# Windowed attention re-ordered into steps of two blocks, ahead of a mixture-of-experts layer, on one Trainium2 core

## The chip, the core and the metric

The kernel runs on one core of one Trainium2 chip. The core has five engines that run on their own and meet at semaphores: PE (TensorE, matmuls and transposes), ACT (ScalarE), DVE (VectorE), POOL (GpSimd) and SP (SyncE, which here only issues transfers). Matmul results land in PSUM, which has eight banks of 512 fp32 columns; operands come from SBUF. The metric is the device time of one execution in microseconds (us).

## What is computed

Four sequences of 768 tokens, eight heads of 64. Each query sees the keys of its last `n_local` = 96 positions and the first `n_global` = 8, with a bias that falls with distance; softmax, then the weighted sum of the values. The 3072 rows of 512 that result go through a cosine router that picks one of eight experts for each row, and the expert's two matmuls.

```python
scores = scale * q @ k.T + bias; a = exp(scores - max); a /= sum(a) + 1e-9
x = (a @ v) as rows of 512                       # 3072 x 512
logits = (x / |x|) @ (emb / |emb|).T / tau       # 8 experts
e = argmax(logits); gate = softmax(logits)[e]
out[row] = gate * (relu(x[row] @ w1[e]) @ w2[e]) # 512 -> 1024 -> 512, fp32
```

## The kernel before, in words

**Attention.** A group is one sequence and four heads (two pairs of heads); there are eight groups, two to a sequence. A unit is one block of 96 keys plus up to 30 global keys (126 rows) against 192 queries; a group has eight units, and there are 64. For each group, `turn` transposes k and q (three transposes into a PSUM bank, one copy by ACT; eight turns for a group). For each unit, `score` issues four matmuls into one tile of two PSUM banks, `sp`, of which there is one; ACT takes the exponential of both banks in one operation (L344); DVE multiplies by a table of biases in two operations (L350). `attend` then adds the values' product into banks `od` (L370) and the sums of the weights into a third (L376, a matmul with ones). After four blocks ACT and DVE copy the three banks out to `xd`.

**Router.** For each of the six row tiles of a sequence (a chunk), `sums` multiplies `xd` with the experts' embedding (L408), transposes the weight sums (L411) and the previous chunk's products (L413), and DVE makes reciprocals and logits of them; `rows` transposes x (L433), DVE scales it, SP stores it to DRAM, ACT squares and sums it. When a sequence is done (the last one in two halves), `choose` finds the expert, the slot of each row, and scatters row numbers and gates to DRAM with six transfers issued by POOL (L202).

**Experts.** For each expert the rows are gathered by number (L643), transposed (L656), multiplied by w1 (L694) and w2 (L666), and scattered to the output (L670).

**What sets the order.** In the attention a scheduler orders the instructions of every engine by priority and readiness, from a program that issues for unit i its scores, one turn of the next group, one router task and the attend of unit i-1. PSUM is divided as two banks for `sp`, four for `od`, two for all else. POOL copies the global rows of v to all eight blocks (L314). All loads go through SP's queue, the first q through ACT's. The program of the experts is issued in the order in which it is written. In the trace each fp32 matmul shows as two rows, so a unit's four score matmuls are eight rows; a transpose is one row.

Of the kernel before, what the change touches and what calls it, by code (L numbers as in the profile page):

```python
# [16 lines left out]
ARMS = (PE, mybir.EngineType.Activation, mybir.EngineType.DVE, mybir.EngineType.Pool)  # L17

# [59 lines left out]
def load_numbers(k, n_global, n_local):  # L78
# [3 lines left out]
    for i, ap in enumerate((n_global, n_local)):  # L82
        nc.scalar.dma_start(raw[:, i, :], ap.bitcast(I32).partition_broadcast(P))
    words = pool.tile([P, 2, 2], F32, name="words")
# [7 lines left out]
    k.ng, k.nl = num[:, 0:1], num[:, 1:2]  # L92

# [12 lines left out]
def prep_expert_emb(k, emb_in, tau, ps):  # L106
# [6 lines left out]
    nc.sync.dma_start(emb[:], emb_in[:, :])  # L113
    sq = pool.tile([E, k.DM], F32, name="emb_sq")
# [4 lines left out]
    nc.gpsimd.tensor_tensor(out=ss[:], in0=ss[:], in1=tau_sb[:], op=ALU.mult)  # L119
    nc.vector.reciprocal(out=ss[:], in_=ss[:])  # L120
    nc.vector.tensor_scalar_mul(emb[:], emb[:], ss[:])
    k.en = pool.tile([P, k.NC, E], F32, name="en")
# [3 lines left out]
    k.enb = pool.tile([P, k.NC, 32], F32, name="enb")  # L126
    nc.gpsimd.memset(k.enb[:], 0.0)
# [5 lines left out]
def load_weights(k, e, w):  # L133
    nc = k.nc
    nc.sync.dma_start(w[0][:], k.w1[e].rearrange("(c p) f -> p c f", p=P))
    nc.sync.dma_start(w[1][:], k.w2[e].rearrange("(f p) m -> p f m", p=P))

# [10 lines left out]
def choose(k, b, i0, n, lg, ss, pool, cp):  # L148
# [21 lines left out]


# [10 lines left out]

    both = new([2, n, E], "both")
# [17 lines left out]
    for t in range(n):  # L201
# [5 lines left out]
        if k.scatters is not None:  # L207
# [3 lines left out]
            k.scatters.append(i.ins)  # L211


def route(k, b, xb, pool):
# [18 lines left out]
    choose(k, b, 0, NT, lg, ss, pool, k.work.tile([P, 512], F32, name="work", tag="work"))  # L233
# [5 lines left out]
def window_table(k, tmp):  # L239
# [9 lines left out]
    rel, far, loc, t = new("rel"), new("far"), new("loc"), new("t")  # L249
# [9 lines left out]
    nc.vector.tensor_scalar(out=t[:], in0=rel[:], scalar1=0.0, scalar2=None, op0=ALU.is_ge)  # L259
    nc.vector.scalar_tensor_tensor(out=loc[:], in0=rel[:], scalar=k.nl, in1=t[:],  # L260
# [13 lines left out]
    for m in range(2):  # L274
        for e in range(2):
            for a in range(2):
                nc.scalar.activation(k.table[:, m, e, a], rel[:], AF.Exp, scale=-k.slopes[4 * m + 2 * a + e])


def window_attention(k, ctx):  # L280
# [71 lines left out]
    def attend(u):  # L352
# [34 lines left out]
        if jj == QB - 1 and n > BLK:  # L387
            g.od = g.od2
# [495 lines left out]
```

## Time and profile before

| | us |
|---|---|
| runs: median of 3 (lowest to highest) | 688.64 (681.72 to 688.98) |
| the profiled execution, its time | 687.63 |
| its span, first to last instruction | 685.8 |
| PE busy in the span | 605.1 (88%) |
| DVE, ACT, POOL busy | 178.6, 141.9, 110.6 |

Times in the profile count from the first instruction. The span has a start (0 to 19.57), the attention proper (to 256.42, the last matmul with the ones), a tail in which the last rows are routed and the first expert's rows gathered (to 297.61), and the experts (to 670.32, the last matmul). A busy PE is not PE at its peak: matmuls are pipelined, and the clock that the chip grants to PE (PEclk) is 1.00 at 2.4 GHz and 0.50 at 1.2 GHz.

### The profile page before, as it was taken

Reading aid. Unit: us, or ns where it says so; the run is one execution under the profiler, and the core shown is the slowest. Engines: PE = TensorE matmul, PEld = TensorE weight load, DVE = VectorE, ACT = ScalarE, POOL = GpSimd, SP = SyncE. Lnnn points to the kernel's source line nnn. Section 1 sums busy time; section 2 is a strip of 40 time slices with the busy share of each in tenths; the row PEclk is TensorE's granted clock in tenths of the full one; section 3 lists DMA queues with packets and bytes.
Section 4 is the critical chain, followed back from the end, with each engine's and each line's share of the span. In section 5 each row is a group of like instructions: output and inputs, shape, how many; then the busy total and the mean of one; then the engine's idle time right before and its main releaser. Section 6 shows DMA issues by size and latency. Waiting matters only on the chain.

```text
span 685.8 us, 8692 instructions
## 1 busy us (share of the span) xinstructions
PE 605.1 (88%) x3314; PEld 338.0 (49%) x3314; DVE 178.6 (26%) x509; ACT 141.9 (21%) x280; POOL 110.6 (16%) x146
## 2 busy tenths in 40 slices
PE   4889998599879984089999999999999999999990
PEld 3556664356546652055456444465564554444540
DVE  3434555255635656011001101001011010020000
ACT  3544552245235431001001011010010100100100
POOL 3110103100310032330130120130301203011010
PEclk9999998979899996579999999999999999999996
DMA  9936783854101028130444150453432535101000
GB/s 228 227 83 153 227 232 90 53 134 106 37 16 47 33 45 293 26 104 1 140 162 169 62 183 1 172 203 141 153 133 80 200 140 174 44 19 48 0 31 22
DMA packets 102685, 75.69 MB, mean 110 GB/s; under 512 B 83441, under 2 KB 83569, under 8 KB 102523
## 3 DMA queue, kind: packets, MB, share of 16 engines
q1 hardware_dynamic: 93610, 58.44, 31.0%
q0 software_dynamic: 5488, 14.71, 5.9%
q8 instruction: 52, 0.85, 0.6%
q10 hardware_dynamic: 3424, 0.79, 0.5%
q14 instruction: 111, 0.90, 0.5%
HBM read 61.11 MB, written 13.59 MB: 109 GB/s over the span
## 4 chain that ended last, share of the span: by engine, by line
PE 56%; DMA 3%; DVE 1%; POOL 1%; issue 0%; ACT 0%; POOLq 0%; SPq 0%; ACTq 0%
PE work L666 27%; PE big L694 25%; PE work L656 2%; DMA x_dram<-xs 1%; DMA meta<-mt,slot 1%; DMA xg<-x_dram,ids 1%; DMA emt<-meta 0%; POOL xg L643 0%; PE tp L433 0%; PE tp L408 0%; PE tp L411 0%; PE od L370 0%; POOL out_dram L670 0%; PE od L376 0%; DVE y L669 0%
## 5 line engine op out<-in xcount | busy, mean ns | idle before, releaser
L666 PE MATMUL work<-w2t,hT 128*128 128x512 f32 x432 | 187.4, 594 | 0.0
L694 PE MATMUL big<-xT,w1t 128*128 128x320 f32 (+5 forms) x512 | 173.6, 500 | 0.8 <-DVE xT L657 0.8
L694 PEld LDWEIGHTS big<-xT,w1t 128*128 128x128 f32 x512 | 98.1, 192 | 76.2 <-issue 42.2
L666 PEld LDWEIGHTS work<-w2t,hT 128*128 128x128 f32 x432 | 81.5, 190 | 101.0 <-issue 99.5
L696 ACT ACTIVATE hT<-big 128x640 f32<-128x640 f32 (+5 forms) x32 | 26.6, 830 | 353.0 <-PE big L694 353.0
L350 DVE TENSOR_TENSOR ex<-ex,table 126x384 f32<-126x384 f32 (+1 forms) x128 | 68.8, 575 | 91.9 <-ACT ex L344 83.8
L670 POOL DMA_INDIRECT out_dram<-y,ids x27 | 26.8, 993 | 301.4 <-DVE y L669 228.7
L340 PE MATMUL sp<-qT,kT 64*126 64x192 f32 (+1 forms) x512 | 67.0, 364 | 7.2 <-ACT qT L328 4.9
L370 PE MATMUL od<-ex,v 126*64 126x192 f32 (+1 forms) x576 | 63.6, 325 | 7.6 <-POOL mt L200 3.8
L669 DVE TENSOR_SCALAR y<-work,emt 128x512 f32<-128x512 f32 x27 | 20.3, 751 | 185.2 <-PE work L666 185.2
L344 ACT ACTIVATE ex<-sp 126x768 f32<-126x768 f32 x64 | 49.2, 768 | 83.9 <-PE sp L340 63.9
L657 DVE COPY xT<-work 128x512 f32<-128x512 f32 x32 | 20.2, 684 | 157.9 <-PE work L656 157.9
L340 PEld LDWEIGHTS sp<-qT,kT 64*126 64x126 f32 x512 | 43.8, 196 | 27.7 <-issue 14.4
L370 PEld LDWEIGHTS od<-ex,v 126*64 126x64 f32 x576 | 35.1, 141 | 27.8 <-issue 16.9
L376 PE MATMUL od<-ex,ones 126*32 126x192 f32 (+1 forms) x576 | 36.7, 318 | 0.7 <-issue 0.7
L656 PE MATMUL work<-ident,xg 128*128 128x128 f32 x128 | 19.0, 295 | 20.7 <-DMA xg<-x_dram,ids 20.7
L643 POOL DMA_INDIRECT xg<-x_dram,ids x32 | 30.9, 966 | 24.0 <-DVE ids L639 14.9
L202 POOL DMA_INDIRECT meta<-mt,slot x24 | 23.9, 996 | 43.9 <-DVE slot L193 19.1
L656 PEld LDWEIGHTS work<-ident,xg 128*128 128x128 f32 x128 | 15.4, 151 | 25.6 <-DMA xg<-x_dram,ids 21.1
L314 POOL COPY v<-v 30x1792 f32<-30x1792 f32 x8 | 13.6, 1706 | 70.5 <-DMA v<-in_v_dram 70.3
L323 PE MATMUL tp<-ident,k 128*128 128x128 f32 x96 | 20.1, 334 | 5.5 <-DMA k<-in_k_dram 5.5
L433 PE MATMUL tp<-ident,xd 128*128 128x128 f32 x96 | 16.4, 299 | 8.8 <-DVE lh L423 8.3
(117 smaller groups left out, 300.3 us busy)
## 6 DMA issues: line engine op xcount, KB each, us to landing
w1t<-in_moe_w_dram SPq DMA_DIRECT2D x8, 2048.0 KB, 9.9
w2t<-in_moe_w_dram SPq DMA_DIRECT2D x8, 2048.0 KB, 12.4
k<-in_k_dram SPq DMA_DIRECT2D x32, 192.0 KB, 3.2
v<-in_v_dram SPq DMA_DIRECT2D x32, 192.0 KB, 3.4
x_dram<-xs SPq DMA_DIRECT2D x24, 256.0 KB, 6.1
q<-in_q_dram SPq DMA_DIRECT2D x28, 192.0 KB, 3.4
q<-in_q_dram ACTq DMA_DIRECT2D x4, 192.0 KB, 4.9
xg<-x_dram,ids POOLq DMA_INDIRECT x32
```

The source lines that it names most:

```text
L202: i = nc.gpsimd.indirect_dma_start(out=k.meta[:], out_offset=bass.IndirectOffsetOnAxis(ap=slot[:, t : t + 1], axis=0), in_=mt[:, t, :], in ...
L340: nc.tensor.matmul(sp[0:ROWS, e, a * n : (a + 1) * n], lhsT=t.kT[rows, j, 0:ROWS], rhs=t.qT[rows, j * BLK : j * BLK + n], start=True, stop ...
L344: nc.scalar.activation(ex, sp[0:ROWS, :, 0 : 2 * n], AF.Exp, scale=k.scale)
L350: nc.vector.tensor_tensor(out=exv, in0=exv, in1=tb, op=ALU.mult)
L370: nc.tensor.matmul(od[a][e * D : (e + 1) * D, cols], lhsT=g.v[0:ROWS, 2 * a + e, j, :], rhs=ex[:, e, a * n + c0 : a * n + c1], start=first ...
L376: nc.tensor.matmul(od[2][32 * i : 32 * i + 32, cols], lhsT=k.ones[0:ROWS, 0:32], rhs=ex[:, e, a * n + c0 : a * n + c1], start=first, stop= ...
L643: nc.gpsimd.indirect_dma_start(out=xg[:], out_offset=None, in_=k.x_dram[:], in_offset=bass.IndirectOffsetOnAxis(ap=ids[:, j : j + 1], axis=0),
L656: k.nc.tensor.transpose(ps[:, c, :], xg[:, c * P : (c + 1) * P], k.ident[:])
L666: nc.tensor.matmul(ps[:], lhsT=hT[:, f, j * P : (j + 1) * P], rhs=w2[:, f, :], start=f == 0, stop=f == k.NF - 1)
L670: nc.gpsimd.indirect_dma_start(out=k.out[:, :], out_offset=bass.IndirectOffsetOnAxis(ap=ids[:, j : j + 1], axis=0), in_=y[:], in_offset=No ...
L694: nc.tensor.matmul(ps[:, i, 0:w], lhsT=w1[:, c, f * P : (f + 1) * P], rhs=xT[:, c, 0:w], start=c == 0, stop=c == k.NC - 1)
L696: nc.scalar.activation(hT[:, 2 * f2 : 2 * f2 + 2, 0:w], ps[:, :, 0:w], AF.Relu)
```

## The change

The attention is written out in steps. One step takes two units: the four matmuls of the first unit's scores, the four of the second, then all transposes that are due (turns, x of a chunk, weight sums), then the attend of the previous step's two units with all products with v first and all products with ones after, then the chunk's product with the embedding. There are 32 steps, four to a group, and some more for what is left of the router. The order of PE, ACT, DVE and SP is that of the program (`manual_schedule`); POOL's is still the scheduler's. PSUM is divided anew: five single banks in rotation for scores, turns and chunks, three for `od`. The exponential is now one operation for each bank, the table's multiplication one for each unit. `choose` and the preparation of the embedding are cut into parts that are issued a step apart. The global rows of v come by transfers from DRAM, and POOL's copies are gone. The first group's k and q are loaded in halves ahead of all else, the bias table is made in two halves, the first expert's weights are loaded in eight parts over steps 9 to 23, and the second expert's weights wait for that expert's row gathers.

```diff
-    sp_p, od_p, tp_p = (pool("wa_sp", 1, space=PSUM), pool("wa_od", 4, space=PSUM),
-                        pool("wa_tp", 2, space=PSUM))
+    pa_p, po_p = pool("wa_pa", 5, space=PSUM), pool("wa_po", 1, space=PSUM)
...
-        nc.gpsimd.tensor_copy(out=d[BLK:ROWS, :, 1:NB, :],
-                              in_=d[BLK:ROWS, :, 0:1, :].to_broadcast([GLB, 4, NB - 1, D]))
+    def load_v(g, hs):
+        for h in hs:
+            src = k.v[g.b, 4 * g.m + h]
+            nc.sync.dma_start(g.v[0:BLK, h], src.rearrange("(j r) d -> r j d", r=BLK))
+            nc.sync.dma_start(g.v[BLK:ROWS, h], src[0:GLB].unsqueeze(1).to_broadcast([GLB, NB, D]))
...
-        nc.scalar.activation(ex, sp[0:ROWS, :, 0 : 2 * n], AF.Exp, scale=k.scale)
+    def grow(u, e):
+        nc.scalar.activation(u.ex[:, e], u.sp[e][0:ROWS, 0 : 2 * u.n].rearrange("p (a c) -> p a c", a=2), AF.Exp,
+                             scale=k.scale)
+
+    def weigh(u):
+        kind = min(u.j, 2)
+        tab = k.table[0:ROWS, u.g.m].rearrange("p e a i c -> p (e a) i c")[:, :, kind::(3 - kind), :]
+        exv = u.ex.rearrange("p e a (i c) -> p (e a) i c", c=BLK)
+        nc.vector.tensor_tensor(out=exv, in0=exv, in1=tab[:, :, 0 : u.n // BLK, :], op=ALU.mult)
...
+    numbers = load_numbers(k, k.n_global, k.n_local)
+    for r0, r1 in ((0, 3), (3, 6)):
+        for a in range(2):
+            load_tokens(nc.sync, first.pairs[a].k, k.k, 0, a, r0, r1)
+            load_tokens(nc.scalar, first.pairs[a].q, k.q, 0, a, r0, r1)
+        if r0 == 0:
+            next(numbers)
...
+            us = g.units[2 * p : 2 * p + 2]
+            for u in us:
+                score(u)
+            grow(us[0], 0)
+            grow(us[0], 1)
+            if s == 0:
+                next(table)
+            weigh(us[0])
+            grow(us[1], 0)
+            todo = list(turns[s])
+            if todo:
+                turn(*todo.pop(0))
+            grow(us[1], 1)
+            for x in todo:
+                turn(*x)
...
+        chunk = ready.pop(0) if ready else None
+        if chunk:
+            t, i = chunk
+            xp = turn_x(t, i) if i < NT else None
+            sp = turn_sums(t, i)
+            if xp is not None:
+                store_x(t, i, xp)
+        if routers:
+            try:
+                next(routers[0])
+            except StopIteration:
+                routers.pop(0)
+        if going:
+            weigh(us[1])
+        if 1 <= s <= 4 * len(groups):
+            q = groups[(s - 1) // 4]
+            attend(q, (s - 1) % 4)
...
+        if chunk and i < NT:
+            score_experts(t, i, sp)
...
-        with ExitStack() as inner:
+        with tc.manual_schedule(engines=ORDERED), ExitStack() as inner:
             window_attention(n, inner)
...
-                load_weights(n, e, t.w)
+                load_weights(n, e, t.w, n.gathers if e == 1 else ())
```

On PE, inside the attention, two units before (`sp`: scores, `od`: products with v and with ones, `tp`: transposes and products with the embedding; counts are matmuls):

```order
L408 MATMUL tp<-xd,enb 32x128 x4
L411 MATMUL tp<-ident,xd 128x128 x2
L413 MATMUL tp<-ident,lS 128x128
L370 MATMUL od<-ex,v 64x192 x4
L376 MATMUL od<-ex,ones 32x192 x4
L340 MATMUL sp<-qT,kT 126x192 x4
L323 MATMUL tp<-ident,k 128x128 x3
L433 MATMUL tp<-ident,xd 128x128 x4
L370 MATMUL od<-ex,v 64x96 x4
L376 MATMUL od<-ex,ones 32x96 x4
```

and one step of the change (`pa`: the five single banks; of the four L421 rows of a full step two stand here):

```order
L395 MATMUL pa<-qT,kT 126x192 x8
L376 MATMUL pa<-ident,k 128x128 x3
L376 MATMUL pa<-ident,q 128x128 x3
L477 MATMUL pa<-ident,xd 128x128 x4
L456 MATMUL pa<-ident,xd 128x128 x2
L458 MATMUL pa<-ident,lS 128x128
L421 MATMUL od_912<-ex,v 64x192 x2
L421 MATMUL od_913<-ex,v 64x192 x2
L429 MATMUL od_914<-ex,ones 32x192 x8
L494 MATMUL pa<-xd,enb 32x128 x4
```

The kinds of matmul now stand in five runs for two units where each unit had four to six runs of its own.

On ACT, at the start, before (`raw`: the numbers n_global and n_local, `table`: the bias table; rows of other copies are left out here and below):

```order
L83 DMA raw_63<-in_n_global_dram 128x2
L83 DMA raw_63<-in_n_local_dram 128x2
L303 DMA q_121<-in_q_dram 128x6x64 x2
L303 DMA q_129<-in_q_dram 128x6x64 x2
L325 COPY kT_125<-tp_173 128x4x96
L328 COPY qT_124<-tp_184 128x384
L277 ACTIVATE table_117<-rel_144 128x384 x8
L328 COPY qT_132<-tp_205 128x384
```

and in the change:

```order
L344 DMA q_109<-in_q_dram 128x3x64 x2
L84 DMA raw_128<-in_n_global_dram 128x2
L84 DMA raw_128<-in_n_local_dram 128x2
L344 DMA q_105<-in_q_dram 128x3x64 x2
L381 COPY qT_110<-pa_250 128x384
L399 ACTIVATE ex_273<-pa_271 126x384
L399 ACTIVATE ex_273<-pa_272 126x384
L309 ACTIVATE table_103<-w_rel_183 128x384 x4
L399 ACTIVATE ex_280<-pa_278 126x384
L381 COPY qT_106<-pa_293 128x384
```

The numbers are now requested behind the first four halves of q, and half of the table is made behind the first unit's exponentials and no longer ahead of the last copies of q.

On POOL, around the first `choose`, before:

```order
L314 COPY v_774<-v_774 30x4x448
L158 TENSOR_TENSOR ss_288<-ss_288,half_244 128x6
L314 COPY v_1096<-v_1096 30x4x448
L200 COPY mt_1850<-tokid_251 128x6
L202 DMA meta_61<-mt_1201,slot_1196 24576x2 x6
L314 COPY v_1425<-v_1425 30x4x448
```

and in the change:

```order
L182 TENSOR_TENSOR ss_265<-ss_265,half_181 128x6
L226 COPY mt_2150<-tokid_220 128x6
L228 DMA meta_61<-mt_1490,slot_1485 24576x2 x6
L182 TENSOR_TENSOR ss_778<-ss_778,half_181 128x6
```

No copy of v stands between the router's instructions on POOL any more.

## Rows read from the trace of the kernel before

**Rows 1.** The page: the chain that ended last, by line.

```profile
PE work L666 27%; PE big L694 25%; PE work L656 2%; DMA x_dram<-xs 1%; DMA meta<-mt,slot 1%; DMA xg<-x_dram,ids 1%; DMA emt<-meta 0%; POOL xg L643 0%; PE tp L433 0%; PE tp L408 0%; PE tp L411 0%; PE od L370 0%; POOL out_dram L670 0%; PE od L376 0%; DVE y L669 0%
```

**Rows 2.** Stretches: start:end length, each engine's busy time (instructions), PEclk, DMA share, GB/s.

```profile
19.57:256.42 236.85, 212.06 (x2162) 132.02 (x2162) 119.67 (x340) 103.31 (x219) 35.42 (x37) 0.94 0.45 104
53.00:78.00 25.00, 25.00 (x281) 15.65 (x277) 12.82 (x26) 12.81 (x28) 1.91 (x1) 1.00 0.75 201
145.00:170.00 25.00, 25.00 (x286) 16.02 (x284) 14.28 (x40) 13.10 (x31) 0.00 (x0) 1.00 0.47 122
205.00:245.00 40.00, 39.93 (x445) 25.12 (x444) 25.57 (x85) 19.71 (x42) 3.86 (x5) 0.99 0.09 34
256.42:297.61 41.19, 12.23 (x71) 8.04 (x67) 15.06 (x86) 3.42 (x12) 11.68 (x13) 0.59 0.52 152
297.61:670.32 372.71, 372.71 (x1058) 192.53 (x1058) 37.40 (x62) 26.57 (x32) 55.83 (x74) 0.99 0.31 107
```

**Rows 3.** Waits of PE in the attention: who for whom, us, times, longest.

```profile
PE tp L433 <- DVE lh L423: 8.3, 1, 8.3
PE od L370 <- POOL mt L200: 3.8, 2, 1.9
PE od L370 <- issue: 3.3, 3, 2.2
```

**Rows 4.** Timeline of ACT: start, length, what, idle before it and its releaser.

```profile
138.08 0.27 ACT L416 COPY lS<-tp 128x128 f32<-128x128 f32 x1 [10.32 <-remote]
```

**Rows 5.** Stretches at the lower clock in the attention: the first, and all five.

```profile
45.47:48.88 3.41, 3.41 (x15) 2.31 (x16) 0.00 (x0) 2.54 (x6) 2.00 (x3) 0.50 0.65 147
...
sum 30.71, PE 25.57 PEld 16.68 DVE 13.87 ACT 12.16 POOL 3.18; mean PE 5.12 PEld 3.33 DVE 2.77 ACT 2.43 POOL 0.64
```

**Rows 6.** Timeline of PE in a dense stretch: start, length, line, form, rows.

```profile
151.21 0.87 PE L370 MATMUL od<-ex,v 126*64 126x192 f32 x8
152.01 0.53 PE L376 MATMUL od<-ex,ones 126*32 126x192 f32 x8
152.47 0.92 PE L340 MATMUL sp<-qT,kT 64*126 64x192 f32 x8
153.32 0.55 PE L323 MATMUL tp<-ident,k 128*128 128x128 f32 x3
153.71 0.60 PE L433 MATMUL tp<-ident,xd 128*128 128x128 f32 x4
154.24 0.55 PE L370 MATMUL od<-ex,v 126*64 126x96 f32 x8
154.72 0.37 PE L376 MATMUL od<-ex,ones 126*32 126x96 f32 x8
155.02 0.39 PE L370 MATMUL od<-ex,v 126*64 126x96 f32 x4
155.34 0.59 PE L340 MATMUL sp<-qT,kT 64*126 64x192 f32 x4
155.86 0.39 PE L370 MATMUL od<-ex,v 126*64 126x96 f32 x4
```

**Rows 7.** Groups of ACT from 145 to 170: busy us, mean ns, idle before.

```profile
L344 ACT ACTIVATE ex<-sp 126x768 f32<-126x768 f32 x7 | 5.7, 807 | 7.6 <-PE sp L340 7.5
L344 ACT ACTIVATE ex<-sp 126x384 f32<-126x384 f32 x1 | 0.5, 471 | 0.0
```

**Rows 8.** Timeline of DVE and ACT at the start: the numbers, the table.

```profile
5.06 0.17 DVE L85 CAST words<-raw 128x4 f32<-128x4 int32 x1 [3.97 <-DMA raw<-in_n_local_dram]
11.52 0.36 DVE L259 TENSOR_SCALAR t<-rel 128x384 f32<-128x384 f32 x1 [5.20 <-POOL rel L254]
15.74 3.41 ACT L277 ACTIVATE table<-rel 128x384 f32<-128x384 f32 x8 [2.94 <-DVE rel L273]
```

**Rows 9.** The chain in order of time, in the tail: start, length, what.

```profile
266.77 10.23 DMA x_dram<-xs
...
277.30 6.71 DMA meta<-mt,slot
```

More of the change, by code (lines that the diff above doesn't have):

```diff
@@ L232, in route @@
         nc.vector.tensor_copy(out=lg[:, t, :], in_=lp[:, 0:E])
-    choose(k, b, 0, NT, lg, ss, pool, k.work.tile([P, 512], F32, name="work", tag="work"))
+    steps = choose(k, b, 0, NT, lg, ss, pool)
+    next(steps)
+    steps.send(k.work.tile([P, 512], F32, name="work", tag="work"))
+    next(steps)
 def window_table(k, tmp):
@@ L334, in score @@
         j, n = u.j, u.n
[L335 removed]
+        u.sp = [bank() for _ in range(2)]
+        u.ex = ex_p.tile([P, 2, 2, 2 * BLK], F32, name="ex", tag="ex")
+        u.ex = u.ex[0:ROWS, :, :, 0:n]
         for a in range(2):
@@ L372, in attend @@
                                      skip_group_check=True)
+        for u, at, c0, c1, first in parts:
             for a in range(2):
@@ L441, in rows, with score_experts @@
         nc.scalar.activation(sq[:], flat, AF.Square, accum_out=t.ss[:, i : i + 1])
-    def finish(t, i0, n):
-        if i0 + n == NT:
-            sums(t, NT)
-        choose(k, t.b, i0, n, t.lg, t.ss, rt_p, bank())
+    def score_experts(t, i, ps):
+        c = slice((i % 3) * P, (i % 3 + 1) * P)
+        for a in range(4):
+            nc.tensor.matmul(ps[32 * a : 32 * a + 32, 3 * P : 4 * P], lhsT=k.enb[:, a, :],
+                             rhs=t.groups[a // 2].xd[i // 3][:, a % 2, c], start=True, stop=True)
+        t.lS[i] = xs_p.tile([P, P], F32, name="lS", tag="lS")
+        nc.scalar.copy(out=t.lS[i][:], in_=ps[:, 3 * P : 4 * P])
+    def finish(t, i0, n):
+        steps = choose(k, t.b, i0, n, t.lg, t.ss, rt_p)
+        next(steps)
+        yield
+        steps.send(bank())
+        yield
+        next(steps)
         if i0 + n == NT:
@@ new lines, in window_attention @@
+    first = groups[0]
+    open_group(first)
+    numbers = load_numbers(k, k.n_global, k.n_local)
+    build_consts(k)
+    for r0, r1 in ((0, 3), (3, 6)):
[4 more added lines that the diff above has]
+            next(numbers)
+    warm = const.tile([P, 1], F32, name="warm")
+    nc.scalar.activation(warm[:], k.ones[:, 0:1], AF.Exp)
+    load_v(first, range(4))
@@ L521, in window_attention, with turns_of @@
-    while tasks:
-        tasks.pop(0)()
+    table = window_table(k, tmp)
+    next(table)
+    next(numbers)
+    next(table)
+    check_numbers(k)
+    build_route_consts(k)
+    for i in (0, 2):
+        for a in range(2):
+            turn(first.pairs[a], i)
+    def turns_of(g, order):
+        return [(g.pairs[a], i) for a in range(2) for i in order]
+    turns = [[] for _ in range(4 * len(groups))]
+    turns[0] = [(first.pairs[a], 3) for a in range(2)]
+    turns[1] = [(first.pairs[a], 1) for a in range(2)]
```

268 lines of the change are left out of this document (136 added, 132 removed).

## The prediction, made before the changed kernel was run

> **What bounds the kernel now.** I read the chain that ended last first. It is PE's work in the experts, L666 and L694, and almost nothing of the attention [rows 1]: the chain is followed back only to where transfers of the tail carry it. So I cut the span into stretches. In the last of them, the experts, PE is busy for all of 372.71 us [rows 2]; nothing there is changed, so these 372.7 us and the 15.5 us behind them stay. The attention takes 236.85 us and the tail 41.19 [rows 2]. What the change can give is in the first 256.42 us.
>
> Is PE the bound there? In three stretches without a wait PE issues 281, 286 and 445 rows in 25, 25 and 40 us [rows 2]: 1012 rows in 90 us, 11.24 a microsecond, at PEclk 1.00 or 0.99. All 2162 rows of the attention at that rate would take 192.3 us. DVE is busy for 0.57 and ACT for 0.52 of the second stretch, so PE is the bound where nothing waits. The other 44.5 us are waits and a slow clock. PE idles 8.3 us for one DVE operation, 3.8 us for `mt` on POOL, 3.3 us for nothing that the profile shows [rows 3]. In 30.71 us PEclk is 0.50, and PE is busy for 25.57 of them [rows 5], which costs half, 12.8 us. These are 28.2 us; about 16 us are many smaller waits.
>
> **The merged runs.** PE's timeline shows that changing from one kind of matmul to another costs time [rows 6]. Eight score rows take 153.32 - 152.47 = 0.85 us, four take 155.86 - 155.34 = 0.52; the second four cost 0.33 and the first four 0.52, so a run costs 0.19 beside its stream. For the products with v, eight rows of 96 columns take 154.72 - 154.24 = 0.48 and four take 155.34 - 155.02 = 0.32: 0.16 a run. For the products with ones, eight rows of 192 take 152.47 - 152.01 = 0.46, of 96 155.02 - 154.72 = 0.30; half of the columns is 0.16, all are 0.32, and 0.14 is left for the run. Three and four transposes in a row take 0.39 and 0.53, 0.92 for seven; the extra one of the second costs 0.14 at most, 0.11 if the run costs 0.15, which I take.
>
> Counts come from the code and from the order that the scheduler made. Scores: 64 runs before, and 8 of them cut in two by an `od` run, so 72; now 32; 40 x 0.19 = 7.6 us. Products with v: ten runs a group, 80, now 32; 48 x 0.16 = 7.7. With ones: nine a group, 72, now 32; 40 x 0.14 = 5.6. Transposes: 64 turns and 24 runs of weight sums behind a product with the embedding, 88, now one a step, 32; 56 x 0.15 = 8.4. The products with the embedding stay 24 runs. Sum 29.3 us, and the dense attention is 192.3 - 29.3 = 163.0. Ends: nothing, if a run of sixteen rows pays at its middle what it paid at its start, and 35 us, if the smaller waits between runs of the old order go too. I take 29.
>
> **What must keep up.** DVE and ACT do the same work in less time: 0.57 x 192.3/163 = 0.67 and 0.52 x 192.3/163 = 0.61. The exponential in two halves costs 2 x 0.471 - 0.807 = 0.135 us more a unit [rows 7], 8.6 us over 64, another 0.05 of ACT. Neither is full, and the products run a step behind their scores, so an exponential has a whole step of about 5 us. I cost the single banks, the split exponential and the five-bank rotation at nothing; PE's own runs hide them. If they were bare, each step would show the ACT time between a score and the reuse of its bank, some 1 us, or 32 us. The parts of `choose` stand on DVE ahead of the second unit's table. One whole `choose` lies in the third stretch, and DVE is at 0.64 there [rows 2], 0.75 after the merge. I take 1 us for each of the four sequences, 4 us; ends 0 and 12.
>
> **The waits.** The 3.8 us for `mt` go: `mt` stands behind the copies of v on POOL, and PE's products with v wait for those copies. Those rows come by 32 more transfers on SP; each also stands ahead of later loads, and DMA is busy for 0.45 of the attention, 107 us [rows 2]. The pieces of 30 x 8 rows are 60 KB each, 1.9 MB in all; at the second row's 201 GB/s for a share of 0.75, 268 GB/s when full, they add 7 us, and 114 us in 163 is 0.70. They are hidden unless loads run late. The waits of PE for `choose` go, because its matmuls are issued a step after their input. With the waits go most of the slow stretches behind them. What I can't explain may come again: the 8.3 us, in which ACT waited 10.32 us for a semaphore that no instruction of the trace set [rows 4], and the 3.3 us. I take half, 6 us, and 3 for the clock behind them; ends 0 and 18. With 4 for `choose` and 2 for loads of the second group that PE may meet in its order, 15 us.
>
> **The start.** Before, the numbers arrived at 5.06, the table's chain ran on DVE from 11.52 (it waited for POOL, which sat behind a copy of v), and ACT made the table from 15.74 to 19.15 [rows 8]; the dense part began at 19.57. Now the numbers are requested behind the first halves of q, and their transfer shares semaphores with those, so I put them 3.5 us later, at 8.5; the DVE chain of 15.74 - 11.52 = 4.2 us then ends near 13.5 with its first operations, half of the table takes 1.7, and the exponentials and q copies behind it 1.8: the second step starts at 17.0 (ends 14 and 20). The first step's 2.3 us of scores and turns are done by then. PE has been mostly idle, so the first microseconds run at the lower clock: 3 us more.
>
> **The tail.** The chain there is copies, chunks, `choose`, POOL's scatters and their landing; the scatter that ends it is issued at 277.30 and lands 6.71 us later [rows 9]. The second expert's weights no longer compete with the last x rows, whose transfer took 10.23 us, but that one ends at 277.00, ahead of the scatter, so I give nothing for it. One chunk more is left behind the last attend, ACT squares x ahead of the copy that the next chunk needs, and the table of slots is no shorter. I keep 41.2; ends 38 and 46. The weights now come behind the second expert's gathers, some 50 us before they are used, which hides them.
>
> **Sum.** Last product with ones: 17.0 + (163.0 - 2.3) + 3 + 15 = 195.7, where it was 256.42: 60.7 us earlier. The profiled execution took 687.63; 687.63 - 60.7 = 626.9, so 627. The median of the runs, 688.64, lies 1 us above it, which changes nothing here.
>
> **The clock, a rule against this change.** The rows first. PE's transposes now stand together, up to thirteen in a run. In the first slow stretch, 15 rows, PEclk is 0.50 [rows 5]; PE did little but turns there, and the clock rose while it did. So here transposes did not hold the clock down. The Trainium skill, "TensorE: Matmul & The Clock Gate", Part 4: PE-mode transpose, says the opposite: a transpose does not count as PE being busy, and the full clock does not engage for it. By that rule longer runs of transposes would let the clock fall in every step. The trace does not agree with it.
>
> **The rivals.** First: the runs merge, but they don't pay, because the price of a run is paid at each new bank. Against it: within a run the rounds follow evenly, and the score rows already change banks within one. Then 627 + 29 = 656. Chance 0.14. The same time comes out if PE must wait 1 us in each step for ACT's bank (32 us, 659); the shares of ACT above speak against it.
>
> Second: loads. SP's queue is in program order now, and each store of x waits for DVE with the next loads behind it. If the last groups' loads come late by the unexplained slow stretch and half as much again, some 16 us, I get 643. Chance 0.10; it lies in the range.
>
> Third, slower: the clock falls in the steps, at the place where thirteen transposes meet the products with v. Each microsecond of dense work at 1.2 GHz costs one more. The gain of 60.7 us is gone when 60.7/163 = 0.37 of the dense work runs at the lower clock, a mean PEclk below 0.73 over the attention. At half of it the time is 627 + 82 = 709. Against it stand the rows on the clock above; it was 0.94 over the old attention. Chance 0.03.
>
> That the order isn't what the code says can be left out: PE's five runs a step stand in the built program.
>
> **The numbers.** My forecast, 610 to 640, has 0.73; the first rival 0.14 (650 to 665), the second 0.10 (640 to 650), the slower one 0.03. Low end: no waits come again (15 less) and the start is 2 us sooner, 627 - 17 = 610. High end: I include the loads and most of the first rival, 657. One per cent, about 7 us, is what a measurement here tells from no change. Faster by over 1% (below 682): 0.95, all cases but the last and what I have not thought of; within 1%: 0.02; slower: 0.03.
>
> **What would show it.** In the profile of the change: PE's last product with ones near 196, against 256.42; stretches of PE without a wait at 2162/163 = 13.3 rows a microsecond; score runs of 16 rows in 0.19 + 4 x 0.33 = 1.5 us; the first dense step near 17; PEclk 1.00 from about 22 on; no PE wait for POOL; the tail near 41 and the experts at 372.7. I am wrong on the merge if a 16-row run takes 1.7, on the overlap if PE's waits for ACT or DVE come once a step, on the loads if PE waits for k or q beyond the first 30 us.

## The result, and the profile after

The changed kernel takes 631.57 us (median of 4 runs, 629.47 to 636.79), the kernel before 685.18 on the same chip (4 runs, 680.33 to 688.98): a ratio of 0.923, 95% interval 0.916 to 0.931. I had forecast 627, with a range of 610 to 657. The profiled execution is the slowest of the four, 636.79 us with a span of 634.8; set against the 626.9 that my sum gives for a profiled execution it is 9.9 us longer, and the steps below are read against that.

The chain that ended last is again the experts, now without a line of the attention but through the last scatter (the page, beside [rows 1]):

```profile
PE work L781 29%; PE big L809 27%; PE work L771 2%; DMA xg<-x_dram,ids 1%; POOL xg L757 0%; POOL out_dram L785 0%; POOL meta L228 0%; DVE y L784 0%; POOLq L792 0%; DVE ids L753 0%; DVEq L993 0%; DVE flags L851 0%; DVE xT L772 0%; POOLq L757
```

The stretches of the new trace, in the columns of [rows 2] (attention from the second step on, two dense stretches, tail, experts):

```profile
15.26:194.90 179.64, 164.50 (x2138) 130.47 (x2137) 105.89 (x251) 104.66 (x284) 21.57 (x23) 0.96 0.84 155
27.00:76.00 49.00, 48.58 (x649) 39.32 (x651) 26.90 (x51) 32.51 (x89) 0.67 (x2) 1.00 1.07 230
122.00:146.00 24.00, 23.97 (x326) 19.46 (x328) 16.17 (x42) 16.30 (x45) 2.30 (x2) 1.00 1.06 190
194.90:247.08 52.18, 15.50 (x93) 10.47 (x86) 20.71 (x111) 4.59 (x18) 18.67 (x21) 0.54 0.22 47
247.08:619.80 372.72, 372.32 (x1058) 192.28 (x1058) 37.84 (x61) 26.57 (x32) 54.61 (x73) 1.00 0.34 118
```

Four things are to be seen. The last product with ones ends at 194.90, 61.5 us earlier than before. The experts take the same 372.7. The tail between them has grown from 41.19 to 52.18 and gives 11.0 us back. In the two dense stretches PE issues 649 and 326 rows, 13.2 and 13.6 a microsecond, where [rows 2] had 11.24.

One step of PE's timeline, in the columns of [rows 6]:

```profile
61.54 1.57 PE L395 MATMUL pa<-qT,kT 64*126 64x192 f32 x16
63.04 0.55 PE L376 MATMUL pa<-ident,k 128*128 128x128 f32 x3
63.42 0.49 PE L376 MATMUL pa<-ident,q 128*128 128x128 f32 x3
63.75 0.60 PE L477 MATMUL pa<-ident,xd 128*128 128x128 f32 x4
64.19 0.38 PE L456 MATMUL pa<-ident,xd 128*128 128x128 f32 x2
64.41 0.27 PE L458 MATMUL pa<-ident,lS 128*128 128x128 f32 x1
64.61 1.20 PE L421 MATMUL od<-ex,v 126*64 126x192 f32 x16
65.74 0.70 PE L429 MATMUL od<-ex,ones 126*32 126x192 f32 x16
66.25 0.40 PE L494 MATMUL pa<-xd,enb 128*32 128x128 f32 x8
66.59 1.33 PE L395 MATMUL pa<-qT,kT 64*126 64x192 f32 x16
```

Each kind of work stands in one run. The length of a run is the distance to the next start: sixteen score rows take 63.04 - 61.54 = 1.50.

What PE waits for between 15 and 195 us, the four longest of seven groups that make 15.1 us (who for whom, us, times, longest), to be set beside [rows 3]:

```profile
PE pa L376 <- ACT lS L497: 7.2, 1, 7.2
PE od L421 <- DVE xd L435: 4.0, 2, 2.0
PE pa L456 <- issue: 1.6, 1, 1.6
PE pa L376 <- ACT ex L399: 1.0, 3, 0.4
```

No wait for POOL is left, and none for k, q or v. The one long wait is of the same sort as in [rows 4]: PE waits for ACT, and ACT for no instruction that the views name (what came late is told with the scatters below).

The start in the timeline of DVE and ACT, and the exponential in halves in the page's groups (beside [rows 8] and [rows 7]):

```profile
7.43 0.17 DVE L87 CAST words<-raw 128x4 f32<-128x4 int32 x1 [4.34 <-DMA raw<-in_n_local_dram]
14.02 1.76 ACT L309 ACTIVATE table<-w_rel 128x384 f32<-128x384 f32 x4
```

```profile
L399 ACT ACTIVATE ex<-pa 126x384 f32<-126x384 f32 (+1 forms) x128 | 53.6, 476 | 30.3 <-PE pa L395 27.6
```

A half costs 476 ns on the mean, where I took 471, and ACT mostly waits for PE, not PE for ACT.

Stretches of the new trace at the lower clock, in the columns of [rows 5]:

```profile
103.25:106.67 3.42, 3.42 (x36) 1.85 (x34) 2.44 (x6) 0.72 (x2) 2.78 (x2) 0.50 0.59 161
151.04:154.45 3.41, 3.41 (x38) 1.82 (x34) 2.54 (x6) 0.72 (x2) 3.06 (x2) 0.50 0.27 84
164.69:171.52 6.83, 3.57 (x21) 3.24 (x23) 1.42 (x4) 2.38 (x7) 0.00 (x0) 0.50 0.00 0
198.83:247.08 48.25, 14.35 (x78) 9.69 (x79) 17.43 (x91) 3.83 (x14) 18.67 (x21) 0.50 0.22 46
```

Each of the first three lies in or right behind a wait of PE of 2.0 or 7.2 us; everywhere else in the dense attention PEclk is 1.00. In the tail the clock stays at 1.2 GHz from 198.83 until the experts run.

The tail in the timeline, first PE, then DVE, POOL and PE again (start, length, what, idle before it and its releaser):

```profile
195.76 0.29 PE L458 MATMUL pa<-ident,lS 128*128 128x128 f32 x1
200.05 0.65 PE L494 MATMUL pa<-xd,enb 128*32 128x128 f32 x8 [4.00 <-DVE lh L466]
202.78 0.66 PE L494 MATMUL pa<-xd,enb 128*32 128x128 f32 x8 [0.39 <-DVE lh L466]
207.16 0.66 PE L494 MATMUL pa<-xd,enb 128*32 128x128 f32 x8 [2.03 <-issue]
...
194.29 0.25 DVE L210 COPY both<-pa 128x96 f32<-128x96 f32 x1
198.70 0.16 DVE L513 TENSOR_TENSOR good<-good,g 128x1 f32<-128x1 f32 x1
198.77 0.55 DVE L435 COPY xd<-od 128x384 f32<-128x384 f32 x1
199.82 0.17 DVE L466 TENSOR_TENSOR lh<-pa,rd 128x64 f32<-128x64 f32 x1
...
223.63 0.96 POOL L228 DMA_INDIRECT meta<-mt,slot  x1 [0.30 <-issue]
235.43 0.99 POOL L757 DMA_INDIRECT xg<-x_dram,ids  x1 [10.84 <-issue]
...
247.08 5.20 PE L809 MATMUL big<-xT,w1t 128*128 128x416 f32 x10 [2.60 <-issue]
```

From 194.29 to 198.77 DVE does the third sequence's last part of `choose`. The copies of `od` and the next chunk's `lh` stand behind it, and PE idles for 4.00 us. The last scatter is issued 223.63 - 194.90 = 28.7 us behind the last product; before it was 277.30 - 256.42 = 20.9 [rows 2, 9].

### The profile page after: what moved, and what is told of

The parts are those of the page before. It is cut to its first block, busy times and chain, and to the rows that moved or that the text cites. A ratio compares the mean times of both kernels' runs of the same rounds, so it can differ in the third digit from the quotient of the medians.

```text
span 634.8 us, 8682 instructions
## 1 busy us (share of the span) xinstructions
PE 559.0 (88%) x3314; PEld 338.6 (53%) x3314; DVE 169.8 (27%) x445; ACT 141.6 (22%) x345; POOL 99.6 (16%) x138
## 4 chain that ended last, share of the span: by engine, by line
PE 59%; issue 2%; POOL 1%; DMA 1%; DVE 0%; POOLq 0%; DVEq 0%
PE work L781 29%; PE big L809 27%; PE work L771 2%; DMA xg<-x_dram,ids 1%; POOL xg L757 0%; POOL out_dram L785 0%; POOL meta L228 0%; DVE y L784 0%; POOLq L792 0%; DVE ids L753 0%; DVEq L993 0%; DVE flags L851 0%; DVE xT L772 0%; POOLq L757 0%
## 5 line engine op out<-in xcount | busy, mean ns | idle before, releaser
L406 DVE TENSOR_TENSOR ex<-ex,table 126x768 f32<-126x768 f32 x64 | 57.9, 904 | 64.2 <-ACT ex L399 59.5
L784 DVE TENSOR_SCALAR y<-work,emt 128x512 f32<-128x512 f32 x27 | 20.3, 751 | 185.2 <-PE work L781 185.2
L772 DVE COPY xT<-work 128x512 f32<-128x512 f32 x32 | 20.2, 685 | 159.3 <-PE work L771 159.3
L399 ACT ACTIVATE ex<-pa 126x384 f32<-126x384 f32 (+1 forms) x128 | 53.6, 476 | 30.3 <-PE pa L395 27.6
L395 PE MATMUL pa<-qT,kT 64*126 64x192 f32 (+1 forms) x512 | 50.6, 336 | 3.4 <-ACT qT L381 3.0
L421 PE MATMUL od<-ex,v 126*64 126x192 f32 (+1 forms) x576 | 47.8, 312 | 4.0 <-DVE xd L435 4.0
L395 PEld LDWEIGHTS pa<-qT,kT 64*126 64x126 f32 x512 | 41.4, 190 | 11.1 <-issue 5.9
L421 PEld LDWEIGHTS od<-ex,v 126*64 126x64 f32 x576 | 35.3, 139 | 12.5 <-DVE xd L435 4.5
L228 POOL DMA_INDIRECT meta<-mt,slot x24 | 26.3, 1094 | 66.9 <-DVE ok L509 21.5
L429 PE MATMUL od<-ex,ones 126*32 126x192 f32 (+1 forms) x576 | 27.5, 315 | 0.0
L376 PE MATMUL pa<-ident,q 128*128 128x128 f32 x96 | 17.2, 297 | 7.8 <-ACT lS L497 7.2
L488 ACT ACTIVATE sq<-xs 128x512 f32<-128x512 f32 x24 | 15.1, 631 | 38.5 <-DVE xs L482 34.0
L376 PE MATMUL pa<-ident,k 128*128 128x128 f32 x96 | 17.2, 296 | 6.0 <-DMA k<-in_k_dram 5.5
```

Of the source, the lines that this page charges most:

```text
L376: nc.tensor.transpose(ps[:, r * P : (r + 1) * P], src[:, 3 * half + r, :, :], k.ident[:])
L395: nc.tensor.matmul(u.sp[e][0:ROWS, a * n : (a + 1) * n], lhsT=t.kT[rows, j, 0:ROWS], rhs=t.qT[rows, j * BLK : j * BLK + n], start=True, st ...
L399: nc.scalar.activation(u.ex[:, e], u.sp[e][0:ROWS, 0 : 2 * u.n].rearrange("p (a c) -> p a c", a=2), AF.Exp, scale=k.scale)
L406: nc.vector.tensor_tensor(out=exv, in0=exv, in1=tab[:, :, 0 : u.n // BLK, :], op=ALU.mult)
L421: nc.tensor.matmul(g.od[a][e * D : (e + 1) * D, at : at + c1 - c0], lhsT=g.v[0:ROWS, 2 * a + e, u.j, :], rhs=u.ex[:, e, a, c0:c1], start=f ...
L429: nc.tensor.matmul(g.od[2][32 * i : 32 * i + 32, at : at + c1 - c0], lhsT=k.ones[0:ROWS, 0:32], rhs=u.ex[:, e, a, c0:c1], start=first, sto ...
```

## The experiments

Kernels in one batch ran on one chip, beside runs of the kernel before. The ratio to before is what can be carried from chip to chip, with intervals of about 0.005 to 0.010 to each side (3 to 7 us).

**The changed kernel once more, merged runs taken apart, choose behind the copies (first batch).** The first kernel is the changed one, unedited.

> The changed kernel itself, unchanged, profiled once more. Theory: its 7.18 us wait of PE for ACT's copy of lS at 167.95 is no part of the program (ACT waited for nothing that the trace shows); here it is missing or stands elsewhere, the profiled span is 627 to 633 in place of 634.8, the tail from the last product with ones to the first expert matmul is again near 52 us, and the median is 631 to 632. Rival: the wait belongs to the order of the program; then it is there again, 7 us at the same step.

Measured: 640.07 us, ratio 0.926 (0.918 to 0.934). The second trace has 197.8 for the attention's end and 53.2 for the tail. The long wait is there again, PE idle for 6.3 us at 169.98 in the same step, and a second one of 2.7 at 117.25. So the rival holds: these waits belong to the program, and only their length changes from run to run.

Products with v and with ones alternate:

```diff
         for u, at, c0, c1, first in parts:
             for a in range(2):
                 for e in range(2):
                     nc.tensor.matmul(g.od[a]...)       # with v
-        for u, at, c0, c1, first in parts:
-            for a in range(2):
                 for e in range(2):
                     nc.tensor.matmul(g.od[2]...)       # with ones
```

> Products with v and with ones alternate by pair of heads: 144 runs of each in place of 32 of each, the same rows. Theory (a run costs 0.16 and 0.14 us beside its stream): 112 x 0.30 = 33.6 us more, 665; the dense rate falls from 13.4 rows a microsecond to about 11. Rival (the runs merged but don't pay, the gain came from fewer waits): within 3 us of the changed kernel, 629 to 635.

Measured: 680.97 us, ratio 0.986 (0.979 to 0.993), 40.9 us more than the changed kernel on the same chip. Its timeline of PE:

```profile
57.95 0.55 PE L421 MATMUL od<-ex,v 126*64 126x192 f32 x4
58.43 0.52 PE L427 MATMUL od<-ex,ones 126*32 126x192 f32 x4
58.88 0.55 PE L421 MATMUL od<-ex,v 126*64 126x192 f32 x4
59.35 0.52 PE L427 MATMUL od<-ex,ones 126*32 126x192 f32 x4
```

Four rows with v take 0.47 to 0.48 and four with ones 0.45. A step with sixteen rows of each and no chunk grows from 4.14 to 5.45 us (from the last row of products with ones in one step to that in the next, both traces), for three more runs of each kind: 0.44 a pair, where I had 0.30. The same rows in more runs give back four fifths of the gain (40.9 of 51.4 us on this chip), so runs cost time, and the rival "they merge but don't pay" falls. With runs as short as four rows a change costs more than I took from runs of four and eight.

Scores of the second block behind the first turn:

```diff
-            for u in us:
-                score(u)
+            score(us[0])
             grow(us[0], 0)
 ...
-            grow(us[1], 0)
             todo = list(turns[s])
             if todo:
                 turn(*todo.pop(0))
+            score(us[1])
+            grow(us[1], 0)
```

> The scores of a step's second block stand behind the step's first turn: 60 runs of scores in place of 32, 66 runs of transposes in place of 38. Theory: 28 x 0.19 + 28 x 0.15 = 9.5 us more, 641. Rival (runs are free): 629 to 635. A second rival (bank waits): the second block's scores come later, so the exponential ends later and PE waits for ACT once a step; then 28 us or more on top.

```profile
58.55 0.92 PE L395 MATMUL pa<-qT,kT 64*126 64x192 f32 x8
59.40 0.55 PE L376 MATMUL pa<-ident,q 128*128 128x128 f32 x3
59.88 0.92 PE L395 MATMUL pa<-qT,kT 64*126 64x192 f32 x8
60.73 0.55 PE L376 MATMUL pa<-ident,k 128*128 128x128 f32 x3
```

Measured: 644.20 us, ratio 0.930 (0.923 to 0.937), 4.1 more than the changed kernel. Undisturbed steps, measured as above, say more than the total: those of 4.14 and 5.13 us take 4.49 and 5.48, 0.35 more for one run of scores and one of transposes, where the sum had 0.19 + 0.15 = 0.34. 28 x 0.35 = 9.8 us; the attention ends only 6.3 later, because the steps in which PE waits for `choose` hide theirs and the standstills differ (the one near 170 has 2.1 us of PE in place of 6.3, the one near 120 more). The rival of free runs falls by the steps, not by the median; that of bank waits falls too.

Each part of `choose` behind the products and the copies of `od`:

```diff
-        if routers:
-            ...
         if going:
             weigh(us[1])
 ...
             score_experts(t, i, sp)
+        if routers:
+            ...
```

> Each part of choose stands behind the step's products and the copies of od, no longer ahead of them on DVE. Theory: PE's waits of 2.0 us for the copies at 102.48 and 150.36 go, and the 3.4 us of half clock behind each, 1.7 us apiece: 7.4 us less, 624; the 4.0 us wait in the tail stays, since the next chunk's sums stand behind the same part on DVE. Rival: the wait only moves (the next step's table products are late and PE waits for those): 629 to 635.

Measured: 637.04 us, ratio 0.921 (0.914 to 0.927), 3.0 less than the changed kernel on that chip, inside the uncertainty. PE's two waits for the copies are gone, and two of 1.3 us for `lh`, behind the same part of `choose` on DVE, have come. The attention ends at 191.1, but the tail is 55.5. The wait is mostly moved.

**The tail, the loads, and what ACT waits for (second batch).** Two chunks in steps 8, 16, 24 and 32:

```diff
+        early = ready.pop(0) if s % 8 == 0 and len(ready) > 1 else None
+        if early:
+            xp = turn_x(*early)
+            esp = turn_sums(*early)
+            store_x(*early, xp)
 ...
+            if early:
+                score_experts(*early, esp)
```

> Two chunks of x are done in every eighth step, so that four chunks stand behind the last products in place of five, and the last part of each choose falls into a step that copies no od. Theory on the tail (52.2 and 53.2 us in the changed kernel, 41.2 before): one chunk, 2.7 us, and PE's wait of 4.0 us behind choose go; tail 45 to 46. The two waits of 2.0 us for the copies and the half clock behind them, 1.7 each, go too: 14 us less in all, a ratio of 0.903 to before where the changed kernel had 0.923 and 0.926. Rival: the tail is set by POOL's scatters and their landing, and what is gained before them is waited for there; then tail 52, ratio 0.92.

Measured: 642.39 us, ratio 0.933 (0.925 to 0.940). The tail is 46.9, near what I expected, but the time is above what both the theory and its rival gave: the last step before the tail is 6.2 us longer, since the chunk and a wait of 2.6 us behind `choose` now stand there, and in the full steps PE waits for DVE's reading of the bank that the extra chunk took (2.1 us, twice, 0.9 once).

The first 30 rows of v copied by POOL again:

```diff
-            nc.sync.dma_start(g.v[BLK:ROWS, h], src[0:GLB].unsqueeze(1).to_broadcast([GLB, NB, D]))
+            nc.sync.dma_start(g.v[BLK:ROWS, h, 0, :], src[0:GLB])
+            nc.gpsimd.tensor_copy(out=g.v[BLK:ROWS, h, 1:NB, :],
+                                  in_=g.v[BLK:ROWS, h, 0:1, :].to_broadcast([GLB, NB - 1, D]))
```

> The first 30 rows of v are loaded once per head and copied seven times by POOL, as before the change; PE's products wait for POOL again, and 60 KB a head come off the queues. My prediction's terms: the 3.8 us in which PE waited for POOL's mt come back, and the transfers were hidden: 4 us more, ratio 0.930. Rival (the DMA share is 1.07 from 27 to 76 us, so the loads were near the limit): less load helps, PE's waits of some 2 us for k and q go, ratio 0.92 or less.

Measured: 643.81 us, ratio 0.934 (0.926 to 0.943). The direction fits my term, but PE waits for POOL nowhere; the standstills alone are 14 us here against 9 in either trace of the changed kernel. So this neither shows nor refutes the 3.8 us.

24 tiny copies more on ACT:

```diff
+            if 4 <= s < 16:
+                for _ in range(2):
+                    nc.scalar.copy(out=warm[:], in_=warm[:])
```

> 24 tiny copies of one column are added on ACT, two in each of the steps 4 to 15, 0.2 us each. In four traces ACT stood still without a cause that the trace shows at its row 215 or 216 and at its row 288 or 289, DVE at its row 161. Theory: the wait goes with the count of ACT's instructions (the next of them are not loaded yet); the waits stand again at rows near 216 and 288, that is two to three steps earlier in the work. Rival: they belong to the place in the program (lS of that step); then they stand at rows near 240 and 312.

ACT's timeline at the first long standstill, in the changed kernel (second trace), where it is ACT's 216th row (waits on semaphores and transfers issued counted too), and with the copies:

```profile
117.86 0.48 ACT L381 COPY qT<-pa 128x384 f32<-128x384 f32 x1 [5.62 <-remote]
```

```profile
119.09 0.33 ACT L399 ACTIVATE ex<-pa 126x192 f32<-126x192 f32 x1 [7.14 <-remote]
```

With the copies it is the 239th row, in the same step. My theory falls: the wait goes with the place in the program, not with the count of ACT's instructions. (640.19 us, one run.) For the other engines the trace of the changed kernel tells the same: from 156.3 to 171.9, across its long standstill, no packet of the queues that load instructions stands in the DMA view. The Trainium skill, "Runtime: NRT & Kernel Launch", section "Instruction fetch mechanics", holds that loading of instructions is mostly hidden; these traces give no reason to doubt it.

Sums in the step of their chunk, with two chunks in every eighth step and `choose` behind the copies:

```diff
-            nc.tensor.transpose(ps[:, 2 * P : 3 * P], t.lS[i - 1][:], k.ident[:])
+            nc.tensor.transpose(ps[:, 2 * P : 3 * P], t.lS[i][:], k.ident[:])
 ...
+        for t, i in (chunks + ready if s > 4 * len(groups) else chunks):
+            if i not in t.lS:
+                score_experts(t, i)
         if going:
```

> Sums are no longer a step behind: the products with the embedding stand at the start of a step, and the same chunk's sums are turned in the same step; two chunks in every eighth step, choose behind the copies of od, the last half's three products with the embedding at once. The chunk that only turned sums is gone, and three chunks stand behind the last products in place of five. Theory: a chunk is worth 2.7 us, PE's wait behind choose 4.0, and the last half's choose starts two steps sooner; last scatter some 12 us sooner, tail 40 to 42; with the copies' waits (2 x 2.0) and their half clock (2 x 1.7) 19 us less, ratio 0.897. Rival (sums in the same step make PE wait for ACT's lS, 0.5 us in 24 steps): 12 us of it given back, ratio 0.914.

Measured: 641.18 us, ratio 0.936 (0.925 to 0.946), above both the theory and its rival. The tail is 44.7, but the products with the embedding, at a step's start, wait for the copies of the step before: 1.0 to 3.7 us, six times in the attention. The sums a step behind earn their place.

**Scatters and choose (third batch).** All traces, that of before too, had standstills behind bursts of scatters, long ones behind some and short ones behind others: before, six were issued from 114.66 to 121.39, and [rows 4] is at 138.08; after, six from 149.02 to 157.27, and PE stood from 160.8 to 168. So the scatters of the first three sequences were left out:

```diff
-    for t in range(n):
+    for t in range(n if b == k.B - 1 else 0):
         i = nc.gpsimd.indirect_dma_start(
             out=k.meta[:], ...
```

> The 18 scatters of slots of the first three batches are left out (their tokens then are empty slots for the experts); the last six stay. In every trace so far PE, ACT and DVE stand still together for 3 to 7 us some 3 to 15 us behind a batch's six scatters (in the changed kernel at 160.8 to 168, six scatters before), and packets of 256 bytes take 2 to 8 us there. Theory: the scatters slow the transfers and with them what the engines wait for; without them the standstills go, the attention ends near 185 in place of 194.9 and 197.8, and the ratio is 0.908 to 0.912. Rival: the standstills have another cause (loads, the order of the program); they stay, ratio 0.923 to 0.926.

The tokens of these sequences then reach no expert; the experts' matmuls are all there and take 373 us. Measured: 620.38 us, ratio 0.903 (0.896 to 0.911), against 0.923 and 0.926. The attention ends at 183.3. Two stretches of the changed kernel's first trace, in the columns of [rows 2]:

```profile
105.00:118.00 13.00, 11.04 (x142) 8.61 (x136) 6.37 (x14) 7.22 (x20) 3.47 (x3) 0.94 1.44 67
160.00:168.00 8.00, 0.82 (x15) 0.66 (x11) 1.30 (x3) 0.99 (x5) 0.00 (x0) 0.79 0.09 33
```

The same stretches without the scatters:

```profile
105.00:118.00 13.00, 13.00 (x184) 10.40 (x178) 7.44 (x16) 8.09 (x23) 0.00 (x0) 0.93 0.64 164
160.00:168.00 8.00, 8.00 (x127) 6.43 (x125) 4.89 (x12) 3.98 (x12) 0.68 (x1) 1.00 0.18 66
```

With the scatters the DMA engines are busy for a share of 1.44 and move 67 GB/s; without, 0.64 and 164. PE has no wait left there but those behind `choose`. So the scatters cause the standstills. The Trainium skill, "DMA: Bandwidth & Descriptors", section "Issuing engines are not separate DMA queues", says that transfers of all issuing engines run on the same 16 DMA engines and interleave; the first pair of rows agrees, since SP's loads slow down behind POOL's scatters. It doesn't explain the second pair, where the DMA engines are nearly idle.

The semaphore events of the traces, which the views above don't print, say what comes late there. In the changed kernel's first trace PE's semaphore is raised at 159.78 and next at 167.61, though the scores that raise it are over by 160.77 by their rows (whose ends are modelled); ACT goes on at 167.63. The completions of a transfer of x whose packets end by 162.32 arrive from 168.28 to 169.19. Without the scatters each such transfer from 140 us to the end of the attention has its last completion within 0.5 us of its last packet, and no such gap stands between PE's events. So what the engines wait for there is the raising of semaphores, PE's and the transfers' alike.

`choose` a step sooner, two chunks in step 32 only:

```diff
+        if chunk:
+            last = t.b == B - 1
+            if last and i == 3:
+                routers.append(finish(t, 0, 3))
+            ...
         if routers:
             ...
```

> The first part of choose runs in the step of its last sums, a step sooner, so that its last part falls into a step that copies no od and, for the third batch, ahead of the last step; and step 32, where no scores are left, does two chunks. Nothing is put into a full step, as it was in the two kernels that lost time there. Theory: PE's waits of 2.0 us for the copies go with their half clock (2 x 3.7), in the tail the 4.0 behind choose and a chunk of 2.7: 14 us less, tail 45 to 46, ratio 0.903 to 0.906. Rivals: choose's last part makes the next step's table products late instead (2 us each time, ratio 0.91), or the tail is set by the scatters' landing (tail 52, ratio 0.915).

```profile
189.37 0.27 PE L458 MATMUL pa<-ident,lS 128*128 128x128 f32 x1
192.27 0.43 PE L494 MATMUL pa<-xd,enb 128*32 128x128 f32 x8 [2.63 <-DVE lh L466]
```

Measured: 637.61 us, ratio 0.931 (0.923 to 0.938); no gain, and above the theory and both rivals. PE's waits for the copies are gone and the tail is 46.6, but a wait of 2.6 us behind `choose` now stands ahead of the last product, and the standstill behind the first burst is 5.4 us of PE. From the products of step 31 to the first expert matmul it takes 56.2 us (from the last row of step 31's products with ones), in the changed kernel 55.4 and 56.5: the shorter tail is work moved ahead of its start.

**Spread scatters (fourth and fifth batch).** One scatter to a step for the first two sequences; DVE makes the slot column in that step, and the scatter waits for it:

```diff
-    for t in range(n):
-        i = nc.gpsimd.indirect_dma_start(... slot[:, t : t + 1] ...)
+    def one(t):
+        at = pool.tile([P, 1], I32, name="slot1", tag="slot1")[:]
+        nc.vector.scalar_tensor_tensor(out=at, in0=best[:, t : t + 1], scalar=float(k.N),
+                                       in1=rank[:, t : t + 1], op0=ALU.mult, op1=ALU.add)
+        scatter(t, at)
+    for t in range(n):
+        if b < 2 and k.scatters is not None:
+            k.late.append(lambda t=t: one(t))
 ...
+        if k.late:
+            k.late.pop(0)()
```

> The six scatters of each of the first two batches go one to a step (a slot column is made by DVE in its step and the scatter waits for it), in place of six in a row of 7.6 us. Without these scatters and the third batch's the ratio was 0.903, and PE, ACT and DVE stood still nowhere. Theory: it is the burst that makes them stand still; spread, a scatter's slow packets are hidden by a step's slack, the standstills go, the attention ends near 185 to 187, ratio 0.905 to 0.912. Rival: each scatter costs its own 1 us or so of standstill wherever it stands; then the attention ends near 195 again, ratio 0.923 to 0.926, with many small standstills in place of two long ones.

```profile
105.00:118.00 13.00, 13.00 (x191) 10.67 (x184) 8.18 (x18) 8.70 (x25) 2.49 (x3) 1.00 1.37 88
160.00:168.00 8.00, 8.00 (x129) 6.45 (x129) 5.86 (x15) 4.86 (x15) 1.77 (x2) 1.00 0.19 66
```

Measured: 631.55 us over 6 runs, ratio 0.919 (0.914 to 0.924): between theory and rival. In the first row the DMA engines are as busy and nearly as slow as with the burst, and PE has no wait: slow loads alone don't stop it. The standstill of the second sequence is gone. Among the first sequence's scatters, where loads still run, PE waits 1.6 us at 123.71 and 3.0 at 138.63. The attention ends at 188.6, 6 to 9 us sooner than in the two traces of the changed kernel. The median ratio is 0.004 to 0.007 lower than its two, less than the intervals can tell.

Both together:

> The scatters spread over steps, choose a step sooner, and two chunks in step 32. Theory: the parts add, since they touch different waits: with spread scatters the attention ended at 188.6 and the first expert began at 243.3; the two waits of 2.0 us for the copies with their half clock (7.4), the 4.0 us behind choose in the tail and a chunk of 2.7 come off that, the first expert begins near 230, the time is 617 to 620 where the changed kernel takes 632, ratio 0.899 to 0.904. Rival: standstills behind the last scatters take the room back, as they did when choose alone was sooner; then 628 to 632, ratio 0.915 to 0.92.

Measured: 628.95 us over 6 runs (623.13 to 632.37), ratio 0.929 (0.924 to 0.934). In its trace the first expert matmul starts at 233.0, 14 to 18 us sooner than in the changed kernel's two, and the tail is 41.4. But that trace is of its fastest run, and the changed kernel's first of its slowest; the ratio is above both the theory and its rival. By the ratios no kernel here that does all of the work is faster than the changed kernel by more than the intervals.

## Why the prediction was right, and where it was not

**The merged runs: right in mechanism and size.** I forecast 13.3 rows a microsecond without a wait; the two dense stretches have (649 + 326)/73 = 13.4. A score run of sixteen rows takes 1.50, as forecast. From 15.26 to 194.90 there are 179.6 us. Waits of 15.1 and 5.2 for the clock (half of the 10.4 us in which PE is busy at 0.50 up to 171.52) leave 159.3 of dense work; I had 163.0 - 2.3 = 160.7. That runs cost time is shown by taking them apart twice. Of the prices, the sum of 0.19 and 0.15 is shown by the steps of the second kernel; a pair of runs of four rows with v and with ones measured 0.44, not 0.30. Counted in the two traces, the runs fall from 75, 82, 73 and 76 (scores, v, ones, transposes) to 32, 32, 32 and 33, where I had 72, 80, 72 and 88: the transposes gave less than I put, and the sum by my prices is 28 us instead of 29.

**The start: a little sooner.** The numbers arrive at 7.43 (I put 8.5), ACT makes the first half of the table from 14.02, and the second step's scores begin at 15.26 (17.0). In [rows 8] the table was made from 15.74.

**The waits: 5 us more than I had, in other parts.** I had 15 us, of it 6 that I could not explain, 4 for `choose`, 2 for loads and 3 for the clock. The trace has 8.8 without a cause that the views name, 4.6 for DVE's copies behind `choose`, 1.7 for ACT's exponentials, none for loads, and 5.2 for the clock, 20.3 in all. The part that I could not explain is the scatters: without 18 of them the standstills are gone.

That the attention ends 0.8 us from my 195.7 is in part luck: these 5.3 us more were made up by a start 1.7 us sooner, by 1.4 us less of dense work, and by the 3 us for a low clock at the start, of which nothing came (PEclk is 1.00 from 14.5 on).

**The tail: wrong, and the whole of the 9.9 us.** The step that failed is "I keep 41.2; ends 38 and 46". It is 52.2 and 53.2. The 11.0 us are 7.8 up to the last scatter (28.7 against 20.9), 1.3 from there to the first gather (11.8 against 10.5, the gather before at 287.81) and 1.9 to the first expert matmul (11.65 against 9.80). Ahead of the last scatter stand PE's wait of 4.0 in the timeline above (I had counted `choose` on DVE at 1 us a sequence and given the tail none) and one chunk more. I had named that chunk and put nothing for it; the distance of two chunks is 202.78 - 200.05 = 2.7. The kernel before took two tasks a unit in the last five units, the changed one takes one chunk a step. A third piece is PE's 2.0 us at 207.16, behind the third sequence's six scatters: without these the wait is gone and the last scatter comes 26.4 us behind the last product. That does not shorten the tail as a whole, which is 51.5 there, so these scatters are not why it grew. The three pieces come to more than the 7.8 (8.7), so they are not an exact account. The wait of 4.0 and the chunk are read from the trace, not shown by a run: three kernels that moved the chunk or `choose` had tails of 44.7 to 46.9, but put work or waits ahead of the last product. What the DVE chain of the last half costs by itself stays open.

**The rivals.** Runs that don't pay: refuted. Loads: my estimate of the DMA share was 0.70, it is 0.84 and 1.07 in the first dense stretch, and still PE waits for no load beyond 30 us. The clock: thirteen transposes stand in a row in the step shown, and PEclk is 1.00 in that stretch. By the rule of the Trainium skill, "TensorE: Matmul & The Clock Gate", Part 4: PE-mode transpose, a transpose does not count as PE being busy in the same way; the clock did not fall here, but a run of 1.6 us between matmuls is all that this trace tests.

## What to carry to other kernels

Price a change of matmul kind from a dense stretch of the timeline, then count runs: here 0.14 to 0.19 us each made an estimated 29 us. The step times bear out the pair of scores and transposes (0.35 for 0.34); in runs of four rows a pair of products cost half as much again (0.44 for 0.30). Do the same for the stretch behind it: work that was taken out of the loop by doing one piece a step comes out at the end, one piece longer, and a block of small DVE operations (4.5 us for `choose`) delays whatever stands behind it on that queue. A wait that the trace can't explain is a term of its own: look at what every such wait follows, and leave that out once. Compare a forecast with its result term by term: here errors of 1 to 5 us cancelled in the attention and hid behind a total that was 0.8 off.

## What the runs showed of the hardware

A burst of six small scatters (128 rows of two numbers each, 8 to 9 us of POOL) can be followed by standstills in which PE idles for up to 8.3 us and ACT for up to 10.3, mostly with DVE, in the kernel before as in the changed one; behind some bursts PE idles for 1 to 2 us only. While loads run, the DMA share rises to 1.44 at 67 GB/s. It also happens with idle DMA engines (share 0.09). 18 scatters cost some 14 us of 632, by the ratios 0.903 against 0.923 and 0.926, give or take 7. What comes late is the raising of semaphores, by PE (7.8 us from one event to the next) and by transfers (6.9 us from the last packet of a transfer of x to its last completion, 0.5 without the scatters in that part of the attention). Why it is held up no row shows; that stays open.
